# Expert blocks of 448 rows for 512, with half-array matmuls for the leftovers, in a fused recurrent and mixture-of-experts kernel

## The chip, the cores and the metric

The kernel runs on one core of a Trainium2 chip. The metric is the device time of one execution in microseconds. Three runs of the kernel before gave 911.64, 923.08 and 937.19 us, median 923.08 us.

## The reference

A recurrent attention block (RWKV-7) runs over 768 steps for 4 batches of 8 heads of 40 dimensions, and its output is taken as 3072 rows of 320. A mixture of 8 experts follows, in which each row goes to one expert.

```python
def _attn_ref(r, k, v, w, a, b):
    ...
    for t in range(S):
        ...
        y[:, :, t] = np.einsum('bhd,bhde->bhe', rt, state)
        Sa = np.einsum('bhde,bhe->bhd', state, at)
        state_decay = state * wt[:, :, None, :] - np.einsum('bhd,bhe->bhde', Sa, bt)
        state = state_decay + np.einsum('bhd,bhe->bhde', vt, kt)
    ...
def _moe_ref(x, w_gate, w1, w2):          # x (3072, 320), w1 (8, 320, 1024), w2 (8, 1024, 320)
    ...
    expert_idx = np.argmax(logits, axis=1)
    ...
        h = np.maximum(x_sorted[lo:hi] @ w1[e], 0.0)
        y_sorted[lo:hi] = h @ w2[e]
    ...
    return (gate_w[:, None] * y)
```

## The kernel before

All data are fp32. The program has three stages.

*Recurrent stage.* The 768 steps are cut into 12 chunks of 64. Each chunk is a chain of small matmuls that use the TensorE array as quarter tiles of 64 x 64 (helper `mm`, L222). The orders of TensorE, VectorE and ScalarE are written out by hand (`weave`); GpSimd and the DMA queues are ordered by the scheduler. At the end of a chunk `emit` multiplies the chunk's outputs by an identity and the gate weights (`ps_x`); ScalarE copies the result to `xr` in two halves (L552), and the sync queue writes 64-row pieces of `xr` to a scratch tensor `x_rows` in memory, 320 columns and one more for the gate weight (L562).

*Routing stage.* VectorE turns the logits into an expert for each row and a slot within the expert. Each expert owns `NJ` = 4 blocks of 128 rows, so its capacity is 512; rows past that go to overflow blocks. A one-hot matmul (`tok_ps`) inverts the slots to lists of row numbers (`g_idx`, `s_idx`), which indirect DMAs on GpSimd use.

*Expert stage.* For each expert: `gather` fetches four blocks of 128 rows from `x_rows` (`xg`, L822); `turn` transposes them on TensorE, three column blocks of 128, 128 and 64 columns (`tp`, L832), with a VectorE copy after each (L833); `layer1` computes eight feature blocks of 128 features, each as three accumulating matmuls over 128, 128 and 64 contraction rows with 512 columns (`hp`, L841), and VectorE and ScalarE take turns at the ReLU (L846, L848); `layer2` makes four output blocks of eight accumulating matmuls of 320 columns (`zp`, L854), ScalarE scales each by the gate weight (`zo`, L859), and GpSimd scatters it to the output (L860). Two experts' weights are in SBUF at a time; `fetch` reads expert e + 2 after expert e is done (L687 w1's first 256 rows, L689 its last 64, L690 w2). The scheduler sets the order of this stage. A last loop handles overflow blocks, as many as the routing has counted.

Of the kernel before, what the change touches and what calls it, by code (L numbers as in the profile page):

```python
# [8 lines left out]
F32 = mybir.dt.float32  # L9
# [12 lines left out]
def kernel(  # L22
# [29 lines left out]
    dch = [(d0, min(128, Dm - d0)) for d0 in range(0, Dm, 128)]  # L52
    DB = len(dch)


    NJ = 4
    CAP = NJ * 128
    NX = -(-(N - CAP) // 128)
    NC = E * NJ + NX
    assert NC <= 128  # L60

# [24 lines left out]
    b1off = counted("b1off", [128, E], [[CAP, E]], -1, 0)  # L86
    b2off = counted("b2off", [128, E], [[-CAP, E]], E * CAP - CAP, 0)
# [28 lines left out]
    x_d = nc.dram_tensor("x_rows", (N, Dm + 1), F32, kind="Internal").ap()  # L116


    with tc.tile_pool(name="ring", bufs=1) as ring, \
# [421 lines left out]
        def emit(us):  # L541
# [3 lines left out]
            xr = sb.tile([128, NB2, NP, 2, D], F32, name="xr", bufs=2)  # L545
            lg = sb.tile([128, 2, NB2, E], F32, name="lg", bufs=2)
            for par, ps in enumerate(pss):
                def end():
# [3 lines left out]
                    nc.scalar.copy(xr[:, :, :, par].rearrange("t s p e -> t (s p) e"), ps[:, :, :, :D].rearrange("t s p e -> t (s p) e"))  # L552
# [143 lines left out]
    with tc.tile_pool(name="rps", bufs=1, space=PSUM) as rps_pool:  # L696
# [9 lines left out]
        xw = x_d[:, Dm : Dm + 1].rearrange("(s b c t) o -> b s t (c o)", b=2, t=64, s=B // 2)  # L706
# [39 lines left out]
        nc.vector.scalar_tensor_tensor(b2[:], in0=b2[:], scalar=128.0, in1=b2off[:], op0=ALU.mult, op1=ALU.add)  # L746
# [16 lines left out]
        nc.vector.tensor_scalar(gx[:], slot[:], scalar1=CAP + 0.5, scalar2=None, op0=ALU.is_ge)  # L763
        nc.vector.tensor_tensor(gx[:], gx[:], b2[:].unsqueeze(2).to_broadcast([128, E, NT]), op=ALU.mult)
# [52 lines left out]
    mps_pool = ctx.enter_context(tc.tile_pool(name="moe_ps", bufs=3, space=PSUM))  # L817

    def gather(g):
        g["xg"] = xg_pool.tile([128, NJ, Dm + 1], F32, name="xg")  # L820
        for j in range(g["n"]):
            nc.gpsimd.indirect_dma_start(  # L822
                out=g["xg"][:, j, :], out_offset=None,
                in_=x_d[:, :], in_offset=bass.IndirectOffsetOnAxis(ap=g["gi"](j), axis=0),
            )

    def turn(g):
        g["xT"] = wk_pool.tile([128, DB, CAP], F32, name="xgT")
        for j in range(g["n"]):
            tp = mps_pool.tile([128, DB, 128], F32, name="tp", bufs=2)  # L830
            for db, (d0, dsz) in enumerate(dch):
                nc.tensor.transpose(tp[:dsz, db, :], g["xg"][:, j, d0 : d0 + dsz], ident[:])  # L832
                nc.vector.tensor_copy(g["xT"][:dsz, db, j * 128 : (j + 1) * 128], tp[:dsz, db, :])  # L833

    def layer1(g):
        cols = g["n"] * 128
        g["h"] = wk_pool.tile([128, FB, CAP], F32, name="h_sb")
        for fb in range(FB):
            hp = mps_pool.tile([128, CAP], F32, name="hp")
# [97 lines left out]
```

## Time and profile before

| | before |
|---|---|
| time, median of three runs | 923.08 us |
| the profiled execution's own time | 923.31 us |
| its span, first to last instruction | 921.6 us |
| TensorE matmuls busy | 793.9 us (86%) |
| TensorE weight loads busy | 599.7 us (65%) |
| VectorE, ScalarE, GpSimd busy | 343.7, 286.2, 368.0 us |
| mean granted TensorE clock | 0.953 of 2.4 GHz |
| mean DMA traffic | 65 GB/s |

The span is one execution seen by the profiler; the time adds what lies before and after it. A matmul's record has a modelled end, so the distance between the starts of two records says more than their durations. One fp32 matmul of the program makes two records, each with its weight load.

### The profile page before, as it was taken

How to read it: one execution, taken by the hardware profiler on the slowest of the kernel's cores; microseconds unless marked ns; L12 is line 12 of the kernel's file. 1: busy time of each engine (PE TensorE's matmuls, PEld its weight loads, DVE VectorE, ACT ScalarE, POOL GpSimd, SP SyncE). 2: the span in 40 equal slices, each digit the busy share in tenths (PEclk: the TensorE clock that was granted, in tenths of full speed). 3: DMA queues.
4: the chain of work that ended last, by engine and by line, in shares of the span. 5: the costliest groups of instructions: out<-in, count | busy, mean ns of one | idle time of the engine just before them, and what ended most of it. 6: DMA issues, size and time to landing. Idle time of an engine off the chain costs nothing.

```text
span 921.6 us, 37467 instructions
## 1 busy us (share of the span) xinstructions
PE 793.9 (86%) x16828; PEld 599.7 (65%) x16828; DVE 343.7 (37%) x645; ACT 286.2 (31%) x756; POOL 368.0 (40%) x436
## 2 busy tenths in 40 slices
PE   0678989898889888888889854999999999999995
PEld 0577988798888788887879852364544545363633
DVE  2467273817374555738363235112010101011100
ACT  0245355435546354554646420101111001111010
POOL 9566355634565555556573326020302021210101
PEclk9999699959999999999999985999999999999998
DMA  4213322312223222322110038032313132221000
GB/s 96 63 40 68 71 45 67 72 45 51 63 62 74 47 62 58 68 61 58 35 33 19 11 74 244 22 142 81 104 65 101 65 100 72 91 80 59 21 0 22
DMA packets 119605, 60.16 MB, mean 65 GB/s; under 512 B 103825, under 2 KB 115091, under 8 KB 119444
## 3 DMA queue, kind: packets, MB, share of 16 engines
q1 hardware_dynamic: 109156, 47.55, 19.9%
q0 software_dynamic: 3072, 9.20, 3.2%
q8 instruction: 133, 2.18, 1.0%
q10 hardware_dynamic: 7216, 1.00, 0.7%
q14 instruction: 28, 0.23, 0.1%
HBM read 49.83 MB, written 9.19 MB: 64 GB/s over the span
## 4 chain that ended last, share of the span: by engine, by line
PE 43%; issue 38%; POOL 9%; DVE 4%; DMA 3%; ACT 1%; SPq 0%; POOLq 0%; DVEq 0%; ACTq 0%
PE ps_lv L222 9%; PE ps_y L222 5%; PE ps_ntb L222 4%; PE ps_q L222 4%; POOL out_dram L860 3%; PE ps_atv L222 3%; PE ps_gtk L222 3%; PE ps_f L222 3%; PE ps_z L222 3%; PE ps_x L222 3%; POOL xg L822 2%; PE ps_S L222 2%; PE ps_uT L222 2%; PE ps_s L222 2%; POOL kb L284 1%
## 5 line engine op out<-in xcount | busy, mean ns | idle before, releaser
L222 PE MATMUL ps_lv<-pair,N 64*64 64x96 f32 (+2 forms) x3840 | 200.3, 243 | 27.4 <-issue 17.9
L222 PEld LDWEIGHTS ps_lv<-pair,N 64*64 64x64 f32 x3840 | 170.3, 137 | 32.9 <-issue 23.1
L841 PE MATMUL hp<-xgT,w 128*128 128x512 f32 (+1 forms) x384 | 191.3, 628 | 0.0
L854 PE MATMUL zp<-w,h_sb 128*128 128x320 f32 x512 | 145.0, 433 | 0.0
L841 PEld LDWEIGHTS hp<-xgT,w 128*128 128x128 f32 (+1 forms) x384 | 63.1, 189 | 122.9 <-issue 120.6
L860 POOL DMA_INDIRECT out_dram<-zo,s_idx x32 | 31.8, 993 | 278.3 <-ACT zo L859 251.2
L854 PEld LDWEIGHTS zp<-w,h_sb 128*128 128x128 f32 x512 | 94.6, 191 | 34.5 <-issue 0.8
L846 DVE TENSOR_SCALAR h_sb<-hp 128x512 f32<-128x512 f32 x32 | 22.1, 692 | 246.5 <-PE hp L841 246.5
L335 DVE STREAM_TRANSPOSE N<-pair 128x512 f32<-128x512 f32 x120 | 84.0, 700 | 64.2 <-ACT pair L385 63.0
L284 POOL TENSOR_TENSOR kb<-kb,wi 128x256 f32<-128x256 f32 x96 | 68.8, 737 | 55.2 <-DVE wi L281 47.7
L222 PE MATMUL ps_ntb<-ai,kb 40*64 40x104 f32 x768 | 64.0, 292 | 28.7 <-POOL ai L275 26.6
L281 DVE RECIPROCAL wi<-PT 128x128 f32<-128x128 f32 x96 | 88.0, 921 | 0.1
L848 ACT ACTIVATE h_sb<-hp 128x512 f32<-128x512 f32 x32 | 19.1, 597 | 198.7 <-PE hp L841 198.7
L385 ACT COPY pair<-ps_lv 128x512 f32<-128x512 f32 x96 | 56.7, 590 | 73.9 <-PE ps_lv L222 58.6
L222 PEld LDWEIGHTS ps_ntb<-ai,kb 40*64 40x64 f32 x768 | 47.3, 157 | 29.2 <-POOL ai L275 26.6
L859 ACT ACTIVATE zo<-zp,xg 128x320 f32<-128x320 f32 x32 | 16.9, 528 | 131.9 <-PE zp L854 128.2
L361 POOL TENSOR_TENSOR pair<-pair 128x256 f32<-128x256 f32 x24 | 17.5, 727 | 89.9 <-DVE pair L355 89.9
L222 PE MATMUL ps_f<-TT,xt 64*64 64x64 f32 x768 | 50.0, 249 | 1.4 <-POOL TT L393 0.9
L549 DVE TENSOR_REDUCE lg<-ps_x 128x16 f32<-128x64 f32 x24 | 5.4, 225 | 118.4 <-PE ps_x L222 115.8
L275 POOL TENSOR_TENSOR ai<-a,PT 128x512 f32<-128x512 f32 x24 | 28.4, 1182 | 51.0 <-DVE PT L271 41.3
L222 PE MATMUL ps_gtk<-ai,kb 40*64 40x104 f32 x768 | 45.4, 262 | 2.4 <-issue 2.4
L222 PE MATMUL ps_atv<-ri,v 40*64 40x104 f32 x768 | 42.2, 255 | 4.9 <-issue 3.9
(170 smaller groups left out, 1548.8 us busy)
## 6 DMA issues: line engine op xcount, KB each, us to landing
w<-in_moe_w_dram SPq DMA_DIRECT2D x8, 1280.0 KB
w<-in_moe_w_dram SPq DMA_DIRECT2D x8, 1024.0 KB
kb<-in_packed_dram SPq DMA_DIRECT2D x176, 40.0 KB
v<-in_packed_dram SPq DMA_DIRECT2D x96, 40.0 KB
wp<-in_packed_dram SPq DMA_DIRECT2D x96, 40.0 KB
ri<-in_packed_dram SPq DMA_DIRECT2D x96, 40.0 KB
x_rows<-xr SPq DMA_DIRECT2D x48, 80.0 KB
a<-in_packed_dram SPq DMA_DIRECT2D x88, 40.0 KB
```

What stands on the lines that cost most here:

```text
L222: nc.tensor.matmul(out_, lhsT=lhs, rhs=rhs, start=start, stop=stop, skip_group_check=free)
L275: nc.gpsimd.tensor_tensor(by_batch(d["ai"][:, :, :T2]), d["a"][:], by_batch(PT[:, :, :T2]), op=ALU.mult,)
L281: nc.vector.reciprocal(wi[:, h, p : p + 2], by_batch(d["PT"][:, :, 1:])[:, h, p : p + 2])
L284: nc.gpsimd.tensor_tensor(d["kb"][:, h, i], d["kb"][:, h, i], wi[:, h], op=ALU.mult)
L335: nc.vector.transpose(N[:].rearrange("q g a t -> q a g t"), nt)
L385: nc.scalar.copy(parts(new[:, :2]), ps[:, :, :T2].rearrange("q g (a t) -> q g a t", a=2))
L822: nc.gpsimd.indirect_dma_start(out=g["xg"][:, j, :], out_offset=None, in_=x_d[:, :], in_offset=bass.IndirectOffsetOnAxis(ap=g["gi"](j), ax ...
L841: nc.tensor.matmul(hp[:, :cols], lhsT=g["w"][0][:dsz, db, fb * 128 : (fb + 1) * 128], rhs=g["xT"][:dsz, db, :cols], start=(db == 0), stop= ...
L846: nc.vector.tensor_relu(g["h"][:, fb, :cols], hp[:, :cols])
L848: nc.scalar.activation(g["h"][:, fb, :cols], hp[:, :cols], AF.Relu)
L854: nc.tensor.matmul(zp[:], lhsT=g["h"][:, fb, j * 128 : (j + 1) * 128], rhs=g["w"][1][:, fb, :], start=(fb == 0), stop=(fb == FB - 1),)
L860: ins_ = nc.gpsimd.indirect_dma_start(out=out[:, :], out_offset=bass.IndirectOffsetOnAxis(ap=g["si"](j), axis=0), in_=zo[:], in_offset=Non ...
```

## The change

An expert now owns three blocks of 128 rows and half a block of 64, so its capacity is 448. The half blocks of two neighbouring experts share one gathered block (`xs`, 128 rows: 64 of each), and the routing has one more step for the slots from 385 to 448. Four things follow.

- `x_rows` is 384 columns wide: its last 64 features stand twice, so that a transposed block has them on partitions 0 to 63 and again on 64 to 127. GpSimd makes the second copy in `xr` before it is written.
- `turn` makes three transposes of 128 columns into one PSUM tile and one VectorE copy of all 384 columns; a shared block is copied in two parts, 64 rows to each expert's `xgT`.
- `layer1` handles feature blocks in pairs with 448 columns. The last 64 contraction rows run as two matmuls, one block on row half 0 to 63 and the other on 64 to 127, into two PSUM banks (`rest`). They come first in pairs 0 and 2 and last in pairs 1 and 3. The weights for them are a tile of their own (`w1r`), with the two blocks' weights on the two halves.
- `layer2` runs for three own blocks, and after every second expert once for the shared block: two matmuls per feature block, one for each expert's 64 rows, with outputs on partitions 0 to 63 and 64 to 127. For this h and w2 have three buffers instead of two.

```diff
-    NJ = 4
-    CAP = NJ * 128
+    NJ = 3
+    OWN = NJ * 128
+    CAP = OWN + 64
+    NO = E * NJ + E // 2
...
+                    nc.gpsimd.tensor_copy(xr[:, :, Dm:], xr[:, :, Dm - 64 : Dm])
                     for s in range(NB2):
                         for b2 in range(2):
...
-                                x_d[r0 : r0 + T2, :Dm], xr[b2 * 64 : b2 * 64 + 64, s].rearrange("t p a e -> t (p a e)"),
+                                x_d[r0 : r0 + T2, :DX], xr[b2 * 64 : b2 * 64 + 64, s],
...
+        t1 = w_pool.tile([128, DF, F], F32, name="w1")
+        tr = w_pool.tile([128, FB // 2, 128], F32, name="w1r")
+        t2 = w_pool.tile([128, FB, Dm], F32, name="w2", bufs=3)
+        for half in range(2):
+            nc.sync.dma_start(
+                tr[half * 64 : half * 64 + 64], w1[DF * 128 :].rearrange("r (q a x) -> a r q x", a=2, x=128)[half],
+            )
...
-        nc.vector.tensor_scalar(gx[:], slot[:], scalar1=CAP + 0.5, scalar2=None, op0=ALU.is_ge)
-        nc.vector.tensor_tensor(gx[:], gx[:], b2[:].unsqueeze(2).to_broadcast([128, E, NT]), op=ALU.mult)
+        gy = sm_pool.tile([128, E, NT], F32)
+        for t, cap, to in ((gx, OWN, b2off), (gy, CAP, b2)):
+            nc.vector.scalar_tensor_tensor(
+                t[:], in0=slot[:], scalar=cap + 0.5, in1=to[:].unsqueeze(2).to_broadcast([128, E, NT]), op0=ALU.is_ge, op1=ALU.mult,
+            )
+        nc.vector.tensor_add(gx[:], gx[:], gy[:])
...
+    def turn(xg, j, *to):
+
+        tp = mps_pool.tile([128, DB, 128], F32, name="tp")
+        for db in range(DB):
+            nc.tensor.transpose(tp[:, db, :], xg[:, j, db * 128 : db * 128 + 128], ident[:])
+        n = 128 // len(to)
+        for i, (xT, c0) in enumerate(to):
+            nc.vector.tensor_copy(xT[:, :, c0 : c0 + n], tp[:, :, i * n : i * n + n])
+
+    def layer1(xT, w, cols):
+        h = wk_pool.tile([128, FB, CAP], F32, name="h_sb", bufs=3)
+        for q in range(FB // 2):
+            hps = [mps_pool.tile([128, CAP], F32, name="hp", bufs=4) for _ in range(2)]
+
+            def rest():
+                for a in range(2):
+                    rows = slice(a * 64, a * 64 + 64)
+                    nc.tensor.matmul(
+                        hps[a][:, :cols], lhsT=w[1][rows, q, :], rhs=xT[rows, DF, :cols], start=(q % 2 == 0), stop=(q % 2 == 1),
+                    )
+
+            if q % 2 == 0:
+                rest()
+            for a in range(2):
+                f0 = (2 * q + a) * 128
+                for db in range(DF):
+                    nc.tensor.matmul(
+                        hps[a][:, :cols], lhsT=w[0][:, db, f0 : f0 + 128], rhs=xT[:, db, :cols],
+                        start=(q % 2 == 1 and db == 0), stop=(q % 2 == 0 and db == DF - 1),
+                    )
+            if q % 2 == 1:
+                rest()
+            nc.vector.tensor_relu(h[:, 2 * q, :cols], hps[0][:, :cols])
+            nc.scalar.activation(h[:, 2 * q + 1, :cols], hps[1][:, :cols], AF.Relu)
+        return h
+
+    def layer2(parts, weight, idx, apart):
+
+        zp = mps_pool.tile([128, Dm], F32, name="zp")
+        n = 128 // len(parts)
         for fb in range(FB):
...
+            for i, (h, w, c0) in enumerate(parts):
                 nc.tensor.matmul(
...
+                    zp[i * n : i * n + n], lhsT=h[:, fb, c0 : c0 + n], rhs=w[2][:, fb, :], start=(fb == 0), stop=(fb == FB - 1),
                 )
...
+    for e in range(E):
+        p = e // 2
         if e + 2 < E:
...
+            if e % 2 == 0:
+                gather_shared(p + 1)
+            gather_own(e + 2)
+        hs[e] = layer1(xTs[e], weights[e], CAP)
         if e + 1 < E:
...
+            if e % 2 == 1:
+                turn_shared(p + 1)
+            turn_own(e + 1)
+        for j in range(NJ):
+            layer2([(hs[e], weights[e], j * 128)], own[e][:, j, DX:], s_idx[:, e * NJ + j : e * NJ + j + 1], True)
+        if e % 2 == 1:
+            layer2(
+                [(hs[i], weights[i], OWN) for i in (e - 1, e)], shared[p][:, 0, DX:],
+                s_idx[:, E * NJ + p : E * NJ + p + 1], True,
+            )
         if e + 2 < E:
             weights[e + 2] = fetch(moe_w1[e + 2], moe_w2[e + 2])
```

How the instructions stand on an engine is the scheduler's work, so three places are shown. A row names the line, the operation, output and inputs, the shape and a repeat count.

TensorE, from the transposes within expert 2's layer two to expert 3's layer one, before (`xg` into `tp` are transposes, `h_sb` into `zp` layer two, `xgT` into `hp` layer one):

```order
L832 MATMUL tp<-ident,xg 128x128 x2
L854 MATMUL zp<-w_11625,h_sb 128x320
L832 MATMUL tp<-ident,xg 128x128 x2
L854 MATMUL zp<-w_11625,h_sb 128x320
L832 MATMUL tp<-ident,xg 64x128 x2
L854 MATMUL zp<-w_11625,h_sb 128x320 x27
L841 MATMUL hp<-xgT,w_11760 128x512 x24
```

And with the change, expert 3's layer one, the transposes for expert 4 (a shared block `xs` and three own blocks) and its own layer two:

```order
L859 MATMUL hp<-xgT,w1r 128x448 x2
L868 MATMUL hp<-xgT,w_11752 128x448 x8
L859 MATMUL hp<-xgT,w1r 128x448 x4
L868 MATMUL hp<-xgT,w_11752 128x448 x8
L859 MATMUL hp<-xgT,w1r 128x448 x2
L846 MATMUL tp<-ident,xs 128x128 x3
L846 MATMUL tp<-ident,xg 128x128 x3
L884 MATMUL zp<-w_11754,h_sb 128x320
L846 MATMUL tp<-ident,xg 128x128 x3
L884 MATMUL zp<-w_11754,h_sb 128x320
L846 MATMUL tp<-ident,xg 128x128 x3
L884 MATMUL zp<-w_11754,h_sb 128x320 x22
```

The 64-row matmuls (L859) now stand as 2, 4 and 2 instead of one in each feature block, the transposes in threes with fewer layer-two matmuls between them, and behind these rows come 16 of the shared block's layer two (`zp`, 64x320), which alternate between expert 2's and expert 3's half.

The sync queue, from the last chunks' writes of `x_rows` to the end of the first weight fetches, before:

```order
L562 DMA x_rows<-xr_10054 64x320 x4
L562 DMA x_rows<-xr_10937 64x320 x4
L687 DMA w1_11315<-in_moe_w1_dram 128x2x1024
L562 DMA x_rows<-xr_11265 64x320 x4
L689 DMA w1_11315<-in_moe_w1_dram 64x1024
L690 DMA w2_11316<-in_moe_w2_dram 128x8x320
L687 DMA w1_11320<-in_moe_w1_dram 128x2x1024
L689 DMA w1_11320<-in_moe_w1_dram 64x1024
L690 DMA w2_11321<-in_moe_w2_dram 128x8x320
```

And with the change (`w1r` is the tile for the last 64 rows):

```order
L570 DMA x_rows<-xr_10951 64x384 x4
L696 DMA w1r_11332<-in_moe_w1_dram 64x4x128 x2
L570 DMA x_rows<-xr_11280 64x384 x4
L699 DMA w1_11331<-in_moe_w1_dram 128x2x1024
L700 DMA w2_11333<-in_moe_w2_dram 128x8x320
L696 DMA w1r_11339<-in_moe_w1_dram 64x4x128 x2
L699 DMA w1_11338<-in_moe_w1_dram 128x2x1024
L700 DMA w2_11340<-in_moe_w2_dram 128x8x320
L700 DMA w2_11615<-in_moe_w2_dram 128x8x320
```

The large w1 piece of expert 0 moved behind the last writes, the small piece ahead of them, and a third w2 joined the first two experts' weights.

GpSimd, at the end of one chunk and the beginning of the next, with the change (`AT` belongs to the chunk's masks, `pair` to the next chunk's first system); before, the same rows stand there without the copy:

```order
L542 TENSOR_TENSOR y<-y,PT_3115 128x512
L330 TENSOR_TENSOR AT_5260<-AT_5260,up_161 128x512
L330 TENSOR_TENSOR AT_5300<-AT_5300,up_161 128x512
L566 COPY xr<-xr 128x2x64
L367 TENSOR_TENSOR pair_5520<-pair_5516 128x256
L368 TENSOR_TENSOR pair_5520<-pair_5520,i_150 128x256
L367 TENSOR_TENSOR pair_5575<-pair_5571 128x256
```

The copy of `xr` came in between the masks and the pair additions.

## Rows read from the trace of the kernel before

**Rows 1.** Table of stretches: busy us per engine (instructions), PEclk, DMA share, GB/s.

```profile
552.00:578.00 26.00, 11.35 (x45) 5.52 (x46) 13.87 (x36) 0.00 (x0) 16.90 (x16) 0.55 0.80 230
704.00:746.00 42.00, 42.00 (x124) 20.55 (x124) 5.69 (x16) 4.51 (x8) 7.50 (x9) 1.00 0.27 86
872.00:921.60 49.60, 39.50 (x109) 19.17 (x108) 2.77 (x4) 4.50 (x8) 4.35 (x5) 0.95 0.03 10
```

**Rows 2.** Page, section 5: the two matmul lines of the expert stage.

```profile
L841 PE MATMUL hp<-xgT,w 128*128 128x512 f32 (+1 forms) x384 | 191.3, 628 | 0.0
L854 PE MATMUL zp<-w,h_sb 128*128 128x320 f32 x512 | 145.0, 433 | 0.0
```

**Rows 3.** Timeline of the sync queue: start, us, then two of the six fetches.

```profile
682.46 0.37 SPq L687 DMA_DIRECT2D w<-in_moe_w_dram  x1
724.78 0.37 SPq L687 DMA_DIRECT2D w<-in_moe_w_dram  x1
```

**Rows 4.** Timeline of PEld: one feature block of layer one, the next's start.

```profile
712.81 0.30 PEld L841 LDWEIGHTS hp<-xgT,w 128*128 128x128 f32 x2 [0.76 <-issue]
713.35 0.19 PEld L841 LDWEIGHTS hp<-xgT,w 128*128 128x128 f32 x1 [0.24 <-issue]
713.78 0.19 PEld L841 LDWEIGHTS hp<-xgT,w 128*128 128x128 f32 x1 [0.24 <-issue]
714.73 0.29 PEld L841 LDWEIGHTS hp<-xgT,w 64*128 64x128 f32 x2 [0.76 <-issue]
715.78 0.30 PEld L841 LDWEIGHTS hp<-xgT,w 128*128 128x128 f32 x2 [0.76 <-issue]
```

**Rows 5.** Timeline of PE, layer two of one expert and what follows it.

```profile
728.85 14.70 PE L854 MATMUL zp<-w,h_sb 128*128 128x320 f32 x54
743.39 6.95 PE L841 MATMUL hp<-xgT,w 128*128 128x512 f32 x14
```

**Rows 6.** Groups of PE by line and shape in the microsecond from 460 us.

```profile
L222 PE MATMUL ps_lv<-pair,N 64*64 64x96 f32 x28 | 1.5, 252 | 0.0
L222 PE MATMUL ps_z<-ri,uT 40*64 40x104 f32 x27 | 1.4, 249 | 0.0
```

**Rows 7.** Timeline of PE, the last chunk's ps_x, first half.

```profile
540.38 0.67 PE L222 MATMUL ps_x<-iw,y 40*64 40x48 f32 x16 [0.17 <-POOL y L536]
```

**Rows 8.** Timeline of VectorE: one routing step, one ReLU, two copies after transposes.

```profile
551.01 0.36 DVE L765 TENSOR_TENSOR slot<-slot,gx 128x192 f32<-128x192 f32 x1
...
721.82 0.69 DVE L846 TENSOR_SCALAR h_sb<-hp 128x512 f32<-128x512 f32 x1 [5.24 <-PE hp L841]
725.05 0.49 DVE L833 COPY xgT<-tp 128x128 f32<-128x128 f32 x2 [2.54 <-PE tp L832]
```

**Rows 9.** DMA view, 563 to 566 us: packets, MB, share; issues, us to landing.

```profile
q1 hardware_dynamic: 776, 0.99, 105.4%
...
xg<-x_rows,g_idx POOLq DMA_INDIRECT x3, 3.8
```

**Rows 10.** DMA view, 566 to 569 us, the same columns.

```profile
q0 software_dynamic: 157, 0.56, 57.4%
q1 hardware_dynamic: 212, 0.25, 22.8%
```

**Rows 11.** Timeline of PE at the start of the expert stage.

```profile
567.99 4.18 PE L832 MATMUL tp<-ident,xg 128*128 128x128 f32 x10 [6.70 <-DMA xg<-x_rows,g_idx]
...
574.38 6.22 PE L841 MATMUL hp<-xgT,w 128*128 128x512 f32 x11
```

**Rows 12.** Timelines of ScalarE and GpSimd after one chunk's last output copy.

```profile
364.71 0.43 ACT L552 COPY xr<-ps_x 128x320 f32<-128x320 f32 x1 [0.18 <-DVE lg L549]
...
367.40 0.73 POOL L361 TENSOR_TENSOR pair<-pair 128x256 f32<-128x256 f32 x1 [4.95 <-DVE pair L355]
```

**Rows 13.** Table of stretches, two in the recurrent stage.

```profile
100.00:104.00 4.00, 4.00 (x78) 4.00 (x78) 0.40 (x2) 1.49 (x4) 0.42 (x1) 0.50 0.02 4
188.00:192.00 4.00, 4.00 (x81) 4.00 (x80) 0.00 (x0) 1.72 (x5) 1.74 (x2) 0.50 0.38 86
```

More of the change, by code (lines that the diff above doesn't have):

```diff
@@ L113 @@
     lmin = rte.tile([128, NT], F32)
-    x_d = nc.dram_tensor("x_rows", (N, Dm + 1), F32, kind="Internal").ap()
+    x_d = nc.dram_tensor("x_rows", (N, DX + 1), F32, kind="Internal").ap()
     with tc.tile_pool(name="ring", bufs=1) as ring, \
@@ L816, with gather @@
     wk_pool = ctx.enter_context(tc.tile_pool(name="moe_wk", bufs=2))
[L817 to L821, printed above, removed]
+    mps_pool = ctx.enter_context(tc.tile_pool(name="moe_ps", bufs=2, space=PSUM))
+    def gather(idx, n, name):
+        xg = xg_pool.tile([128, n, DX + 1], F32, name=name)
+        for j in range(n):
             nc.gpsimd.indirect_dma_start(
-                out=g["xg"][:, j, :], out_offset=None,
-                in_=x_d[:, :], in_offset=bass.IndirectOffsetOnAxis(ap=g["gi"](j), axis=0),
-            )
@@ L827, in turn @@
[L827 to L837, printed above, removed]
+                out=xg[:, j, :], out_offset=None,
@@ new lines, in layer2 @@
+        zo = wk_pool.tile([128, Dm], F32, name="zo", bufs=3)
+        nc.scalar.activation(zo[:], zp[:], AF.Copy, scale=weight)
+        ins_ = nc.gpsimd.indirect_dma_start(
+            out=out[:, :], out_offset=bass.IndirectOffsetOnAxis(ap=idx, axis=0),
+            in_=zo[:], in_offset=None, bounds_check=N - 1, oob_is_err=False,
+        )
+        ins_ = getattr(ins_, "ins", ins_)
+        if apart:
+            tc.declare_no_dep(ins_, group="rows_out", reason="disjoint rows")
+            tc.add_to_no_dep_group("rows_out", ins_)
@@ L869, in cols_of, with gather_own, gather_shared @@
     def cols_of(t, c0):
         return lambda j: t[:, c0 + j : c0 + j + 1]
-    groups = [dict(n=NJ, gi=cols_of(g_idx, e * NJ), si=cols_of(s_idx, e * NJ), apart=True) for e in range(E)]
-    gather(groups[0])
-    gather(groups[1])
-    turn(groups[0])
-    for e, g in enumerate(groups):
+    own, shared, xTs, hs = {}, {}, {}, {}
+    def gather_own(e):
+        own[e] = gather(cols_of(g_idx, e * NJ), NJ, "xg")
+    def gather_shared(p):
+        shared[p] = gather(cols_of(g_idx, E * NJ + p), 1, "xs")
@@ L877, with turn_own, turn_shared @@
+    def turn_own(e):
+        for j in range(NJ):
+            turn(own[e], j, (xTs[e], j * 128))
+    def turn_shared(p):
+        for e in (2 * p, 2 * p + 1):
+            xTs[e] = wk_pool.tile([128, DB, CAP], F32, name="xgT", bufs=3)
+        turn(shared[p], 0, (xTs[2 * p], OWN), (xTs[2 * p + 1], OWN))
+    gather_shared(0)
+    gather_own(0)
+    gather_own(1)
+    turn_shared(0)
+    turn_own(0)
+    for e in range(E):
+        p = e // 2
         if e + 2 < E:
-            gather(groups[e + 2])
@@ L879 @@
-        g["w"] = weights.pop(e)
-        layer1(g)
+            if e % 2 == 0:
+                gather_shared(p + 1)
+            gather_own(e + 2)
+        hs[e] = layer1(xTs[e], weights[e], CAP)
         if e + 1 < E:
-            turn(groups[e + 1])
-        layer2(g)
+            if e % 2 == 1:
+                turn_shared(p + 1)
+            turn_own(e + 1)
+        for j in range(NJ):
+            layer2([(hs[e], weights[e], j * 128)], own[e][:, j, DX:], s_idx[:, e * NJ + j : e * NJ + j + 1], True)
@@ L897 @@
             )
-            g = dict(n=1, w=w, gi=lambda j: gi[:, 0:1], si=lambda j: gi[:, 1:2], apart=False)
-            gather(g)
-            turn(g)
-            layer1(g)
-            layer2(g)
+            xg = gather(lambda j: gi[:, 0:1], 1, "xs")
+            xT = wk_pool.tile([128, DB, CAP], F32, name="xgT", bufs=3)
+            turn(xg, 0, (xT, 0))
+            h = layer1(xT, w, 128)
+            layer2([(h, w, 0)], xg[:, 0, DX:], gi[:, 1:2], False)
 _OUTS = [((3072, 320), 'float32')]
```

67 lines of the change are left out of this document (21 added, 46 removed).

## The prediction

> **What bounds the kernel now.** I read the table by stage first. From 578 to 912 us, the expert stage, TensorE is busy in every microsecond at a granted clock of 1.00, while VectorE, ScalarE and GpSimd are busy for 5.7, 4.5 and 7.5 of 42 us and the DMA engines for 0.27 of it [rows 1]. Six starts of a weight fetch stand 42.3 us apart, one expert each [rows 3]: eight experts fill 339 of the 921.6 us, and each is a chain of TensorE work with nobody else late. So here columns streamed are time, and the page's two costly groups say which ones: 384 records of layer one and 512 of layer two [rows 2], two records for each fp32 matmul (8 x 24 and 8 x 32 matmuls). The recurrent stage before it is not touched but for one copy.
>
> Next, the price of one record. In layer one the weight loads of a feature block start at 712.81, 713.35, 713.78, 714.73 and the next block at 715.78 [rows 4]: 0.43 us from one 512-column record to the next, 2.97 us a block. Six records are 6 x 0.43 = 2.57 us, so 0.39 us of each block is lost at the two places where the loads change between 128 and 64 rows: 0.2 us a change. In layer two 54 records of 320 columns lie between 728.85 and 743.39: 0.269 us each [rows 5]. Both are 0.84 ns a column. One expert is then 8 x 2.97 = 23.7 (layer one) + 64 x 0.269 = 17.2 (layer two) + 1.4 us of transposes, the rest of 42.3.
>
> **The change, part by part.** (a) *Layer one, 448 columns for 512.* A record becomes 448/512 x 0.43 = 0.376 us. The 32 records that contract all 128 rows cost 12.0 us. (b) *The last 64 rows.* Sixteen records on 64 rows now come as pairs, one on each row half. If a pair takes the time of one: 8 x 0.376 = 3.0 us; if the halves run one after the other, 6.0. The expert stage of before has no such pair, but the recurrent stage has a stricter case: in the microsecond from 460 us, 55 records of 96 and 104 columns overlap [rows 6]. Taking off the 10 or so that began before it, 45 x some 84 ns = 3.8 us of streaming was done in 1.0 us, so four quarter tiles ran at once, among them tiles that share their columns and differ in rows. I take 3.0. (c) *Fewer changes of shape.* The order gathers the 64-row records of the second and third pair of blocks, so an expert has 6 changes for 16: 1.2 us. Layer one: 12.0 + 3.0 + 1.2 = 16.2 for 23.7.
>
> (d) *Layer two.* Three own blocks are 48 x 0.269 = 12.9 us. The shared block is 32 records for two experts, in two column halves. As pairs they are 16 x 0.269 = 4.3 us, one after the other 8.6; a change of shape adds 0.2. The row for column halves of the same rows is ps_x: 16 records of 48 columns in 0.67 us [rows 7], of which some 0.22 is the tail of the last. That is 7 steps of 0.06 us for pairs, where two records alone would need 0.08 and a perfect pair 0.04. With such short records I put the missing 0.02 down to the weight loads, which a 0.269 us record covers, and take 4.3; half of 4.5 is 2.25 us an expert. Layer two: 15.2 for 17.2.
>
> (e) *Transposes.* 10.5 for 12 an expert, no longer cut to 64 columns, and one copy for three. A copy of 384 columns lies between those of 128 (0.245 us) and 512 (0.69) [rows 8], about 0.57; with two buffers the third turn may wait 0.2 us for the first copy behind the last ReLU. I leave the 1.4 us as they are (1.0 to 2.2).
>
> One expert: 16.2 + 15.2 + 1.4 = 32.8 us, a gain of 9.6, eight times 76.6. What might be late next is not: weights are 2.6 MB an expert, at the 0.33 MB/us seen in [rows 9] 8 us out of 32.8; VectorE and ScalarE keep about 5 us each, and GpSimd issues 7 transfers for 8.
>
> (f) *Start of the expert stage.* The third w2 buffer lets the sync queue issue expert 2's w2 (1.31 MB) with the first weights, and the big part of expert 0's w1 (1.05 MB) now stands behind the last x_rows writes, where a 0.26 MB part stood. So 2.1 MB more lie in the hardware queue when the first gather is issued at 563. In the trace that queue (q1) moved 0.99 MB in the 3 us after 563 and the gathers' queue (q0) has no line there [rows 9]; their packets appear only in the next 3 us, when the weights end with 0.25 MB [rows 10], and the first transpose waits for them until 567.99 [rows 11]. If gathers stand behind weights, they come 2.1/0.33 = 6.4 us later. Against that, the turns that took from 567.99 to 574.38, before layer one streams [rows 11], have six copies instead of twelve, about 4 us instead of 6.4. The sum lies between -2.4 (gathers not held) and +6 (held, and the turns no faster); I take +4, as [rows 9] and [rows 10] say that they are held. The Trainium skill (DMA: Bandwidth & Descriptors, Queues, rings and completion order) says that each DMA engine goes round between the queues that have work, packet by packet; by that the gathers would not be held, and the total would be some 6 us lower; [rows 9] does not agree.
>
> (g) *Recurrent stage.* Twelve GpSimd copies of 128 columns, each behind ScalarE's xr copy, with the pair add queued behind it. After one xr copy ends at 365.14, GpSimd idles until 367.40 [rows 12], and the gap is 2.1 us or more in all twelve chunks, against some 0.4 us for a copy (half of a 256-column operation of 0.73 there). The writes of x_rows wait for it, but nobody waits for those until the gathers. Zero; uncovered it would be 12 x 0.4 = 5 us. (h) *Routing.* Three VectorE operations on 192 columns for two, 0.36 us each [rows 8]: +0.4. The overflow loop stays empty: the reference's own inputs give each expert 323 to 423 rows, and the new capacity is 448.
>
> **Sum.** The profiled execution took 923.31 us (span 921.6 and 1.7 around it), 0.2 above the median of the three runs, so I sum against it: 923.3 - 76.6 + 4 + 0.4 = **851 us**.
>
> **Rivals.** *Row halves do not overlap.* The 64-row pairs would cost 3.0 us more an expert: 851 + 24 = 875. For it: no 64 x 128 pair stands in the trace, and both halves feed all 128 columns. Against it: [rows 6]. *Column halves do not overlap:* 4.3 us more for each of four shared blocks, 868; for it, that both halves read the same rows; against it, [rows 7]. *Halves overlap in part.* If the 1.5 of [rows 7] (0.06 for 0.04) holds for long records too, the shared blocks cost 2.15 x 4 = 8.6 and the row pairs 1.5 x 8 = 12 us more: 872. For it: it is the only row of this very form. Against it: [rows 6], and the weight loads explain it. Of this rival the Trainium skill has a measured case (TensorE: Matmul & The Clock Gate, Measured speedup vs the span model): four row tiles gave 3.07 instead of 4. An estimate by that ratio, a pair at 1.3 of one record, is 863; no run here shows it for long records.
>
> *Slower: the clock.* The recurrent stage, which runs on half and quarter tiles, has stretches at a granted clock of 0.50 (1.2 GHz) with TensorE busy in all of it [rows 13]; the expert stage held 1.00 on full tiles. If its half-tile parts made the clock fall, each microsecond of full-speed work at half clock costs one more. Of the stage's 260 us, 72 at half clock eat the gain and some 90 make the kernel over 2% slower (941 or more); all of it would give over 1100. Against it: only 5.3 of 32.8 us an expert are half tiles, in pairs that fill the array.
>
> **How the numbers follow.** The forecast as worked out has 0.79, the row rival 0.05, the column rival 0.05, partial overlap 0.07, the slow clock 0.02, and 0.02 something that leaves the time within 2%. Around 851 the forecast's own spread is the start term (-6 to +2), the turns (-3 to +6), and above all the recurrent stage: the profiled run has two stretches of 20 us or more at half clock, of which [rows 13] shows 4 us each, and one more or fewer moves a run by some 10 us, as the three runs from 912 to 937 show. That makes 836 to 866 for it. Held to 8 in 10, with most of the column case: **836 to 869**. A measurement of this kernel can tell about 2% from no change; faster by more than that (below 905): 0.96, within 2%: 0.02, slower: 0.02.
>
> **What the profile after would show.** Weight fetches of experts about 32.8 us apart, on the mean of an odd and an even one (30.5 and 35). In layer one 448-column records 0.376 us apart, and in the 64-row parts two starts within some 10 ns and then 0.376 us. If those starts stand alone at 0.376, the row rival is right. In the shared block, two 320-column starts every 0.269 us; 0.4 speaks for partial overlap. Between the blocks, no TensorE wait over 0.3 us except at the third turn. At the start, the first transpose near 574 and layer one streaming from about 578; if it comes at 568, (f) was wrong. GpSimd's xr copy must end before the pair add would have started. The forecast fails if the stage is still 40 us an expert, if TensorE waits for the gather or the weights in each expert, or if PEclk in the expert stage is below 1.00.

## The result and the profile after

The changed kernel took 846.87 us in the median of four runs (836.65 to 850.72), the kernel before 927.85 us in the four beside them (911.64 to 937.19). The ratio is 0.919 with a 95% interval of 0.898 to 0.941: faster. In two further sets of runs it was 0.910 (0.901 to 0.920; medians 831.01 and 909.39 us) and 0.912 (0.907 to 0.918; 828.54 and 911.01 us). The forecast was 851 us, in a range of 836 to 869.

The profiled execution after took 844.75 us (span 843.0), against 923.31 before: 78.6 us less. The first view is the page's list of groups: line, operation, busy us and mean ns of one record, idle time before.

```profile
L884 PE MATMUL zp<-w,h_sb 128*128 128x320 f32 (+1 forms) x512 | 124.1, 433 | 0.0
...
L868 PE MATMUL hp<-xgT,w 128*128 128x448 f32 x256 | 101.4, 549 | 0.0
```

Layer two has the 512 records that it had before [rows 2], and yet 21 us less busy time at the same 433 ns of one: 128 of them, those of the four shared blocks, now run in pairs. Layer one's full-row records are 256, of 448 columns for 512. To see where an expert's time goes, I read the timeline of TensorE over two experts in the steady stage; columns are start, us, line, operation, count.

```profile
639.83 1.02 PE L859 MATMUL hp<-xgT,w1r 64*128 64x448 f32 x4
640.78 6.28 PE L868 MATMUL hp<-xgT,w 128*128 128x448 f32 x16
646.99 1.77 PE L859 MATMUL hp<-xgT,w1r 64*128 64x448 f32 x8
648.69 6.28 PE L868 MATMUL hp<-xgT,w 128*128 128x448 f32 x16
654.90 1.02 PE L859 MATMUL hp<-xgT,w1r 64*128 64x448 f32 x4
655.86 0.87 PE L846 MATMUL tp<-ident,xg 128*128 128x128 f32 x6
656.57 0.70 PE L884 MATMUL zp<-w,h_sb 128*128 128x320 f32 x2
657.11 0.54 PE L846 MATMUL tp<-ident,xg 128*128 128x128 f32 x3
657.49 12.55 PE L884 MATMUL zp<-w,h_sb 128*128 128x320 f32 x46
669.96 1.02 PE L859 MATMUL hp<-xgT,w1r 64*128 64x448 f32 x4
...
685.04 1.02 PE L859 MATMUL hp<-xgT,w1r 64*128 64x448 f32 x4
...
688.57 16.47 PE L884 MATMUL zp<-w,h_sb 128*128 128x320 f32 x76
704.97 1.02 PE L859 MATMUL hp<-xgT,w1r 64*128 64x448 f32 x4
```

No row carries an idle time, and no record starts more than 0.48 us behind the one before it: TensorE waits for nobody. Layer one lasts from 639.83 to 655.86, 16.0 us (forecast 16.2). Eight 64-row records take 1.77 us and four 1.02, so the four between them cost 0.75: two steps of 0.376 us for two pairs (the two starts of a pair lie 7 ns apart, as the trace has them). In layer two 46 own records last 12.55 us; at the end of the odd expert 76 records, 44 own and 32 of the shared block, last 16.47. The 44 are 44 x 0.269 = 11.8 us, and the shared block has 4.6 left (forecast 4.5 with its change of shape). The sync queue's fetches show the same in whole experts; before, they stood 42.3 us apart [rows 3].

```profile
655.00 0.37 SPq L699 DMA_DIRECT2D w<-in_moe_w_dram  x1
...
685.14 0.37 SPq L699 DMA_DIRECT2D w<-in_moe_w_dram  x1
...
720.15 0.37 SPq L699 DMA_DIRECT2D w<-in_moe_w_dram  x1
...
750.29 0.37 SPq L699 DMA_DIRECT2D w<-in_moe_w_dram  x1
```

They are 30.14, 35.01 and 30.14 us apart: 32.6 an expert in the mean (forecast 30.5 and 35.0, mean 32.8). The table of stretches gives the clock and the other engines over these two experts, in the columns of [rows 1].

```profile
639.83:704.97 65.14, 65.14 (x247) 36.60 (x246) 8.60 (x16) 8.05 (x15) 13.81 (x15) 1.00 0.38 118
```

TensorE is busy in all of it at 1.00 (2.4 GHz), and nobody else is near: in these two experts the slow clock of the prediction did not come, and no wait took the place of the streamed columns.

The start of the expert stage is where forecast and trace part. Below are TensorE's timeline there, the table of stretches from layer one's first record to 577 us, the gathers' rows of GpSimd, then the DMA view of 561 to 564 us and that of 564 to 567 us (packets, MB, share; issues, us to landing).

```profile
568.65 0.88 PE L846 MATMUL tp<-ident,xs 128*128 128x128 f32 x3 [8.70 <-DMA w<-in_moe_w_dram]
...
573.31 1.87 PE L859 MATMUL hp<-xgT,w1r 64*128 64x448 f32 x4
```

```profile
573.31:577.00 3.69, 3.69 (x8) 1.58 (x8) 0.56 (x1) 0.00 (x0) 2.78 (x4) 0.50 0.63 164
```

```profile
562.28 1.19 POOL L836 DMA_INDIRECT xs<-x_rows,g_idx  x1 [2.79 <-DMA w<-in_moe_w_dram]
563.77 0.95 POOL L836 DMA_INDIRECT xg<-x_rows,g_idx  x1 [0.30 <-issue]
```

```profile
q1 hardware_dynamic: 848, 1.09, 106.3%
...
xs<-x_rows,g_idx POOLq DMA_INDIRECT x1, 6.3
```

```profile
q1 hardware_dynamic: 862, 1.09, 107.3%
```

The gathers are held behind weights, as forecast: q0 has no line in either view, and the first gather lands 6.3 us after its issue. But the first transpose comes at 568.65, where I had put 574, and layer one streams from 573.31, where I had put 578; before, these were 567.99 and 574.38 [rows 11]. That row leaves out what ran between the two:

```profile
572.11 2.05 PE L841 MATMUL hp<-xgT,w 128*128 128x512 f32 x2
```

Two records of layer one stood before the last two transposes (at 573.95), so before, 1.84 us of layer one's work lay ahead of 574.38. Both kernels begin layer one at a granted clock of 0.50: after until 577.0, before from 572.11 to 575.5. The weights named behind "<-" can't be what was waited for: this transpose reads gathered rows alone, and a gather reads none of the weights.

Last, the recurrent stage: GpSimd's new copy behind one chunk's xr copy.

```profile
360.52 0.29 POOL L566 COPY xr<-xr 128x128 f32<-128x128 f32 x1 [2.12 <-ACT xr L559]
362.72 0.73 POOL L367 TENSOR_TENSOR pair<-pair 128x256 f32<-128x256 f32 x1 [1.91 <-DVE pair L361]
```

The copy takes 0.29 us, and after it GpSimd still waits 1.91 us for VectorE. It lies in the gap of [rows 12] and costs nothing.

The 78.6 us split at two marks, the last normalized logits on VectorE and the start of layer one's streaming. The recurrent stage up to the first mark ends 1.65 us earlier (542.27 for 543.92), the start takes 31.04 us for 30.46, and the expert stage to the end of the span 269.7 for 347.2: -1.65 + 0.58 - 77.53 = -78.6. With the 1.84 us of layer one counted in both kernels to the expert stage, the start is 2.4 us longer and the expert stage 79.4 us shorter.

### The profile page after: what moved, and what is told of

The parts are those of the page before. It is cut to its first block, busy times and chain, and to the rows that moved or that the text cites. A ratio compares the mean times of both kernels' runs of the same rounds, so it can differ in the third digit from the quotient of the medians.

```text
span 843.0 us, 37380 instructions
## 1 busy us (share of the span) xinstructions
PE 709.9 (84%) x16816; PEld 576.3 (68%) x16816; DVE 332.9 (39%) x582; ACT 282.6 (34%) x752; POOL 364.4 (43%) x442
## 3 DMA queue, kind: packets, MB, share of 16 engines
q8 instruction: 133, 2.18, 1.1%
## 4 chain that ended last, share of the span: by engine, by line
PE 48%; issue 35%; POOL 7%; DVE 4%; DMA 4%; ACT 1%; SPq 1%; POOLq 0%; ACTq 0%; DVEq 0%
PE ps_lv L228 11%; PE ps_y L228 6%; PE ps_ntb L228 5%; PE ps_q L228 4%; PE ps_atv L228 4%; PE ps_gtk L228 3%; POOL out_dram L889 3%; PE ps_f L228 3%; PE ps_z L228 3%; PE ps_x L228 3%; PE ps_S L228 2%; PE ps_uT L228 2%; PE ps_s L228 2%; POOL xg L836 1%; DMA w<-in_moe_w_dram 1%
## 5 line engine op out<-in xcount | busy, mean ns | idle before, releaser
L884 PE MATMUL zp<-w,h_sb 128*128 128x320 f32 (+1 forms) x512 | 124.1, 433 | 0.0
L889 POOL DMA_INDIRECT out_dram<-zo,s_idx x28 | 27.9, 998 | 210.3 <-ACT zo L888 209.7
L884 PEld LDWEIGHTS zp<-w,h_sb 128*128 128x128 f32 (+1 forms) x512 | 80.5, 177 | 37.1 <-issue 2.4
L874 DVE TENSOR_SCALAR h_sb<-hp 128x448 f32<-128x448 f32 x32 | 20.0, 625 | 209.3 <-PE hp L868 132.3
L868 PE MATMUL hp<-xgT,w 128*128 128x448 f32 x256 | 101.4, 549 | 0.0
L228 PE MATMUL ps_ntb<-ai,kb 40*64 40x104 f32 x768 | 62.4, 288 | 28.9 <-POOL ai L281 26.9
L868 PEld LDWEIGHTS hp<-xgT,w 128*128 128x128 f32 x256 | 47.8, 192 | 53.1 <-issue 53.1
L875 ACT ACTIVATE h_sb<-hp 128x448 f32<-128x448 f32 x32 | 17.4, 544 | 142.8 <-PE hp L868 87.6
L888 ACT ACTIVATE zo<-zp,xg 128x320 f32<-128x320 f32 x24 | 12.7, 528 | 100.0 <-PE zp L884 100.0
L228 PEld LDWEIGHTS ps_f<-TT,xt 64*64 64x64 f32 x768 | 42.0, 144 | 2.8 <-issue 1.1
```

The costliest lines, as they stand in the source:

```text
L228: nc.tensor.matmul(out_, lhsT=lhs, rhs=rhs, start=start, stop=stop, skip_group_check=free)
L868: nc.tensor.matmul(hps[a][:, :cols], lhsT=w[0][:, db, f0 : f0 + 128], rhs=xT[:, db, :cols], start=(q % 2 == 1 and db == 0), stop=(q % 2 == ...
L874: nc.vector.tensor_relu(h[:, 2 * q, :cols], hps[0][:, :cols])
L875: nc.scalar.activation(h[:, 2 * q + 1, :cols], hps[1][:, :cols], AF.Relu)
L884: nc.tensor.matmul(zp[i * n : i * n + n], lhsT=h[:, fb, c0 : c0 + n], rhs=w[2][:, fb, :], start=(fb == 0), stop=(fb == FB - 1),)
L888: nc.scalar.activation(zo[:], zp[:], AF.Copy, scale=weight)
```

## The experiments

Totals of this kernel move by 10 us and more between executions. The reading that does not is the expert stage: from layer one's first record to the end of the span it took 269.7, 269.9 and 269.7 us in the three traces of the changed kernel, while their spans were 843.0, 830.8 and 830.3. So each experiment is read by that length and by the spacing of its fetches, and totals stand beside.

**Row halves.** Both matmuls of a 64-row pair run on row half 0 to 63:

```diff
-        tr = w_pool.tile([128, FB // 2, 128], F32, name="w1r")
+        tr = w_pool.tile([64, 2, FB // 2, 128], F32, name="w1r")
...
-                tr[half * 64 : half * 64 + 64], w1[DF * 128 :]...
+                tr[:, half], w1[DF * 128 :]...
...
-                    rows = slice(a * 64, a * 64 + 64)
+                    rows = slice(0, 64)
...
-                        hps[a][:, :cols], lhsT=w[1][rows, q, :], ...
+                        hps[a][:, :cols], lhsT=w[1][rows, a, q, :], ...
```

> Both 64-row matmuls of each pair on row half 0 to 63 (the second half's weights and columns are read from there too); the output is then another one. Theory (row halves run at the same time, a pair for 0.376 us): the pair parts now need 16 records in turn for 8, +3.0 us an expert; fetch starts 33 and 38 us apart for 30.1 and 35.0, total +24, about 869. In the records, the two starts of a pair 0.376 us apart for 0.007. Rival (the gain of layer one comes from the columns and the order alone, the halves run in turn anyway): spacing unchanged, about 845.

The computation is the whole one, other than this says: xgT holds the last 64 columns in both row halves. The timeline of TensorE over one layer one:

```profile
664.51 1.77 PE L859 MATMUL hp<-xgT,w1r 64*128 64x448 f32 x4
666.21 6.28 PE L868 MATMUL hp<-xgT,w 128*128 128x448 f32 x16
672.42 3.27 PE L859 MATMUL hp<-xgT,w1r 64*128 64x448 f32 x8
675.62 6.28 PE L868 MATMUL hp<-xgT,w 128*128 128x448 f32 x16
681.83 1.77 PE L859 MATMUL hp<-xgT,w1r 64*128 64x448 f32 x4
```

The pair parts, 1.02, 1.77 and 1.02 us in the changed kernel, are 1.77, 3.27 and 1.77: 3.0 us more, and nothing else moved. The spacing is 33.1 and 37.95, and the stage 294.3 us, 24.6 longer, for 24 expected (the single total is 854.07 us, beside 904.41 of the kernel before). The theory holds to the 0.376 us step; the rival falls.

**Column halves.** In the shared block one expert's 8 matmuls come before the other's:

```diff
-        for fb in range(FB):
-            for i, (h, w, c0) in enumerate(parts):
+        for i, (h, w, c0) in enumerate(parts):
+            for fb in range(FB):
```

> In the shared block the 8 matmuls of one expert's column half come before the other's 8, no longer by turns; the output is the same. Theory (column halves overlap only because the two records stand next to each other): +4.3 us for each of four shared blocks, odd spacing 39 for 35.0, even 30.1, total +17, about 862. Rival (the halves do not overlap in the changed kernel, or overlap whatever the order): spacing unchanged, about 845.

This run took 985.09 us, and its table of stretches says why it can't be used: the first stretch lies in the recurrent stage, which the edit doesn't touch, the second in the expert stage.

```profile
100.00:400.00 300.00, 299.97 (x8776) 297.21 (x8772) 151.68 (x251) 140.96 (x382) 151.18 (x163) 0.65 0.26 58
...
640.00:940.00 300.00, 300.00 (x832) 142.22 (x831) 28.60 (x53) 27.36 (x51) 39.47 (x40) 0.75 0.22 71
```

So the kernel was run again, in four executions:

> The kernel with the column halves of the shared block in turn, once more, as its first run had a granted clock of about 0.7 from the recurrent stage on (985 us). Theory (the low clock belonged to that run, since it began 500 us before the changed block): granted clock about 0.96, odd spacing 39.3 for 35.0, even 30.1, total +17 on the changed kernel of the same chip. Rival (the order in turn brings the low clock with it): again 0.7 and 950 or more, in most of the executions. Rival on the halves: odd spacing unchanged at 35.0.

The granted clock was 1.00 this time (575 to 743 us of the profiled execution), and no execution came near the 985 us: that rival falls. From the timeline of TensorE, then of the table of stretches for zp alone (us, TensorE busy and records, weight loads busy and records; then ScalarE, clock, DMA):

```profile
677.13 19.75 PE L884 MATMUL zp<-w,h_sb 128*128 128x320 f32 x76
```

```profile
691.00:692.00 1.00, 1.00 (x5) 0.55 (x4) 0.00 (x0) 1.00 0.44 164
692.30:693.30 1.00, 1.00 (x9) 0.67 (x8) 0.00 (x0) 1.00 0.29 60
694.00:695.00 1.00, 1.00 (x5) 0.55 (x4) 0.00 (x0) 1.00 0.66 148
```

The 76 records take 19.75 us for 16.47. Odd spacing is 38.28, even 30.14, the stage 283.0 us, 13.3 longer: the column halves overlap in the changed kernel, and to alternate them saves 3.28 us a block. That is 1.0 less than the 4.3 expected, and the table shows where it is: about four weight loads begin in a microsecond in the middle of either half, but eight at the seam. There the second expert's first four records run beside the first's last four, 4 x 0.269 = 1.08 us, though the kernel's text has them behind (the order in which the scheduler put them on the engine is not on record for this run). The total was 853.87 us in the median beside 828.54 of the changed kernel on that chip, more than 13.3 explains; its executions had a mean granted clock of 0.946 to 0.970 against 0.963 to 0.976. What made up the rest, and what set the low clock of the first run, stays open.

**Changes of shape.** The 64-row pair always stands first in its pair of feature blocks:

```diff
-                        ..., start=(q % 2 == 0), stop=(q % 2 == 1),
+                        ..., start=True, stop=False,
...
-            if q % 2 == 0:
-                rest()
+            rest()
...
-            if q % 2 == 1:
-                rest()
```

> The pair of 64-row matmuls stands first in each of the four pairs of feature blocks: 8 changes between 128 and 64 rows an expert for 6 within layer one. Theory (0.2 us a change): +0.4 us an expert, fetch starts about 30.5 and 35.4 apart, total +3. Rival (the 0.2 us belongs to 64-row records that stand alone and not to the change): nothing, 30.1 and 35.0.

The fetches of two experts, big part of w1 again:

```profile
655.34 0.37 SPq L699 DMA_DIRECT2D w<-in_moe_w_dram  x1
...
685.88 0.37 SPq L699 DMA_DIRECT2D w<-in_moe_w_dram  x1
...
721.28 0.37 SPq L699 DMA_DIRECT2D w<-in_moe_w_dram  x1
```

30.54 and 35.40 us: +0.40 and +0.39, two changes of 0.2 us each. The stage is 273.0, 3.3 longer for 3.2 expected; the rival falls (the single total is 845.95 us).

**The two parts alone.** One kernel has the row-half pairs with four own blocks of 128 rows, the other the 448 columns and the shared block with layer one's order as it was. The first also has the old routing and two buffers of w2 and h, which go with four blocks:

```diff
-    NJ = 3
+    NJ = 4
     OWN = NJ * 128
-    CAP = OWN + 64
-    NO = E * NJ + E // 2
+    CAP = OWN
+    NO = E * NJ
...
```

```diff
...
+        for fb in range(FB):
+            hp = mps_pool.tile([128, CAP], F32, name="hp", bufs=4)
+            for db in range(DB):
+                r = 128 if db < DF else 64
+                nc.tensor.matmul(
+                    hp[:, :cols], lhsT=w[0][:r, db, fb * 128 : (fb + 1) * 128], rhs=xT[:r, db, :cols],
+                    start=(db == 0), stop=(db == DB - 1),
+                )
...
```

> Only the layer-one part of the change: row-half pairs and their grouping, with four own blocks of 128 rows an expert (512 columns), no shared block. Theory by the terms of the sum at 512 columns: 32 records x 0.43 = 13.7, 8 pairs x 0.43 = 3.4, 6 changes 1.2, layer two 17.2, turns 1.4: 36.9 us an expert for 42.3, total 923 - 8 x 5.4 = 880. Rival (pairs run in turn): 40.3 us an expert, about 907.

> Only the other part: three and a half blocks (448 columns) with the shared block in column halves; layer one's last 64 rows as before, one 64-row matmul within each feature block. Theory by the terms: 48 records x 0.376 = 18.0, 16 changes 3.2, layer two 15.2, turns 1.4: 37.8 us an expert for 42.3, total 923 - 8 x 4.5 = 887. Rival (column halves run in turn): 40.0 us, about 905.

> The changed kernel once more on this chip, for the comparison with its two parts: 845 +- 10 us, spacing 30.1 and 35.0. The two parts' gains should add up to the whole's, but for what they share: 43 (pairs) + 36 (blocks) against 77, as 448 columns also shorten the pairs and the pairs shorten the 448 columns.

Fetch starts of the pairs alone, then of the blocks alone:

```profile
706.96 0.37 SPq L698 DMA_DIRECT2D w<-in_moe_w_dram  x1
...
744.07 0.37 SPq L698 DMA_DIRECT2D w<-in_moe_w_dram  x1
```

```profile
659.11 0.47 SPq L694 DMA_DIRECT2D w<-in_moe_w_dram  x1
...
694.15 0.47 SPq L694 DMA_DIRECT2D w<-in_moe_w_dram  x1
...
734.25 0.47 SPq L694 DMA_DIRECT2D w<-in_moe_w_dram  x1
```

Pairs alone: 37.11 us an expert (36.9 expected). Blocks alone: 35.04 and 40.10, 37.6 in the mean (37.8). Both rivals, 40.3 and 40.0, fall. Totals are 866.69 and 875.68 us in the median beside 909.39 before and 831.01 after (the 845 +- 10 expected for the last was too high, as the kernel before took 14 us less here than in the runs that the forecast was made from), ratios to before 0.953 (0.944 to 0.961) and 0.961 (0.949 to 0.974). The pairs save 5.2 us an expert and the blocks 4.7, together 9.9, and the whole 9.7. What they share is then 0.2 us; by the terms it should be 0.43, 8 x (0.43 - 0.376), as the pairs stream 448 columns only in the whole. I did not follow the difference.

**The start.** Expert 2's w2 is taken out of the first weights, with two buffers for three; in a second kernel expert 1's weights also go out on GpSimd's queue behind the first gathers:

```diff
-        t2 = w_pool.tile([128, FB, Dm], F32, name="w2", bufs=3)
+        t2 = w_pool.tile([128, FB, Dm], F32, name="w2")
```

```diff
...
-    weights = {e: fetch(moe_w1[e], moe_w2[e]) for e in range(2)}
+    weights = {0: fetch(moe_w1[0], moe_w2[0])}
...
     gather_own(1)
+    weights[1] = fetch(moe_w1[1], moe_w2[1], nc.gpsimd)
     turn_shared(0)
```

> w2 has two buffers for three, so expert 2's w2 is not among the first weights but is fetched when expert 0 is done. Theory for the start of the expert stage (gathers are held behind what is left on the hardware queue): 1.3 MB less is in front of them, about 4 us at 0.33 MB an us; the first transpose comes near 565 for 568.65, if the x_rows writes end at the same time. Rival (only some 5 us of holding whatever is queued): first transpose within 1 us of 568.65. In the steady stage both expect the even and odd spacing unchanged at 30.1 and 35.0 while the fetch of w2 (4 us) has 30 us to land; if spacing grows, the third buffer hides a wait.

> Expert 1's weights go out on GpSimd's queue behind the first three gathers, and w2 has two buffers; only expert 0's weights are on the hardware queue when the gathers are issued. Theory (gathers wait for the queued weights): first transpose 3 to 4 us earlier than 568.65, total about -3. Rival (holding does not depend on what is queued): no change at the start. Price to watch in both: expert 1's weights must land by about 603, some 40 us after their issue.

With two w2 buffers, the first gather on GpSimd, then on TensorE the first transposes and those of the fifth block:

```profile
545.42 1.19 POOL L836 DMA_INDIRECT xs<-x_rows,g_idx  x1 [2.43 <-DVE s_idx L826]
```

```profile
549.23 0.87 PE L846 MATMUL tp<-ident,xs 128*128 128x128 f32 x3 [5.78 <-DMA xs<-x_rows,g_idx]
...
553.91 0.87 PE L846 MATMUL tp<-ident,xg 128*128 128x128 f32 x3 [0.39 <-DMA xg<-x_rows,g_idx]
```

And the DMA view of 547 to 550 us there:

```profile
q0 software_dynamic: 139, 0.45, 58.2%
q1 hardware_dynamic: 35, 0.04, 3.6%
```

The first transpose begins 3.8 us after the gather's issue, against 6.4, 5.9 and 5.2 in the three traces of the changed kernel: 1.31 MB less is worth 1.4 to 2.6 us of holding, not the 4 expected. The second kernel shows why no more was to be had. There the hardware queue is empty when the first gather is issued, and the transpose still comes 3.7 us behind it: that is what a gather takes here with nothing in front.

From the last normalized logits to layer one it is 28.9 us against 31.0, 30.0 and 31.7; the single total is 826.01 us. Of what the first transpose gained, part is lost again: the gathers are issued 1.25 us apart, and once they are not held, each block's transposes wait for its own gather, down to the fifth block's in the row above (the turns take 5.5 us for 4.7). Spacing is 30.14 and 35.01 as expected, the stage 269.5, so the third buffer hides nothing here. In the second kernel the gathers were issued 21.3 us after the logits (20.0, 22.4 and 20.0 in the three traces of the changed kernel, 19.6 with two buffers), and layer one begins after 30.5. Nothing is won: 829.91 us in the median beside 831.01.

**A version meant to beat both.** Two w2 buffers, and layer one over 424 columns:

```diff
-    CAP = OWN + 64
+    CAP = OWN + 40
...
-    b3off = counted("b3off", [128, E], [[-64, E]], E * 64 - 64, 0)
+    b3off = counted("b3off", [128, E], [[-64, E]], E * 64 - 40, 0)
...
-        h = wk_pool.tile([128, FB, CAP], F32, name="h_sb", bufs=3)
+        h = wk_pool.tile([128, FB, OWN + 64], F32, name="h_sb", bufs=3)
+        if cols == CAP:
+            nc.gpsimd.memset(h[:, :, CAP:], 0.0)
```

> A version meant to beat both: layer one over 424 columns for 448 (the fullest expert of these inputs has 423 rows; beyond 424 the overflow loop takes them), the 24 unused columns of h set to zero by GpSimd, and two w2 buffers for three. Theory (column streaming sets the expert): 24 x 0.84 ns x 40 record times = 0.8 us an expert, spacing 29.3 and 34.2, 6.4 us in all; with the start some 2 us earlier as with two w2 buffers alone, 8 us or 1.0% below the changed kernel. Rival (a part of each record does not go by its columns, or the ReLUs and buffers end last): spacing gain under 0.4 us.

> The changed kernel on the same chip and in the same rounds, to stand beside the two others: spacing 30.1 and 35.0, ratio to before about 0.91 to 0.92.

```profile
664.78 0.37 SPq L699 DMA_DIRECT2D w<-in_moe_w_dram  x1
...
698.96 0.37 SPq L699 DMA_DIRECT2D w<-in_moe_w_dram  x1
...
728.27 0.37 SPq L699 DMA_DIRECT2D w<-in_moe_w_dram  x1
```

These fetch starts are 34.18 and 29.31 us apart, 0.83 less each, as 24 columns at 0.84 ns ask. The stage is 263.9 us, 5.8 shorter for 6.4 expected (layer one's first 5.2 us ran at a granted clock of 0.50, its first 3.7 in the run beside), and it starts 28.6 us after the logits for 30.0. The totals say less: 824.87 us in the median (ratio to before 0.909, 0.904 to 0.914) beside 828.54 (0.912, 0.907 to 0.918). The traces say 7 us of gain, the medians 3.7, and the intervals overlap. It is faster than the kernel before; that it beats the changed kernel is shown in the stage that it changes and not in the totals.

## Why the prediction was right, and where it was off

- **(a) and (b), layer one's columns and pairs.** The 448-column records stream in 0.376 us, and a pair of row halves takes the time of one record. Shown by the timeline after, and by the run on one row half, which cost the 3.0 us an expert that the row rival was priced at.
- **(c) Changes of shape.** 0.2 us each, shown by two more of them costing 0.40. Layer one came to 16.0 for 16.2.
- **(d) Layer two.** The shared block takes 4.6 us for 4.5. The column rival falls with the run in turn; its price, 4.3 us, was too high by the 1.0 that the halves still overlap at the seam. The partial overlap is out too: [rows 7] gave 1.5 for short records, and the stage lost nothing of it with records of 0.269 us. The Trainium skill (TensorE: Matmul & The Clock Gate, Measured speedup vs the span model) has four row tiles at 3.07 instead of 4; here two row tiles of 448 columns give 2.
- **(e) Transposes.** The expert's remainder is 32.6 less layer one's 16.0 and layer two's 15.2 (12.9 and half of 4.6): 1.4 us, as taken. No turn waited in the two experts shown.
- **(f) The start: the term that was mis-sized.** "I take +4" came to +2.1 for the same work (the 2.4 above less the routing), and by the prediction's own sign, a first transpose at 568, (f) was wrong. The mechanism was there: the gathers stand behind the hardware queue. The step that failed is that "2.1 MB more lie in the hardware queue when the first gather is issued". The DMA view from that issue on, 563 to 575 us before and 562.28 to 574 us after, has what was left in the queue (packets, MB, share):

```profile
q1 hardware_dynamic: 988, 1.24, 32.0%
```

```profile
q1 hardware_dynamic: 1640, 2.06, 52.0%
```

It is 0.8 MB more. Of the 2.1, 0.8 was expert 0's w1 piece, which only changed places: before, it was issued at 543.77 us, 0.15 ahead of the last logits, and went out ahead of the gathers too. Of the 1.4 MB that were really added (w2 and the wider rows), 0.6 had already been moved (4.89 MB between the logits and the first gather for 4.33). So the first transpose came 6.4 us after the gather's issue for 5.0, +1.4 and not +6.4.

The turns were to save 2.4 us by six copies for twelve. The 6.4 us that the prediction read from [rows 11] hold the two records of layer one, so twelve transposes took 4.55; after, they took 3.83 (568.65 to 572.48), 0.7 less, and then the scheduler had put three transposes of expert 1's first block ahead of layer one, 0.8 us. The first gather left 0.6 us later behind its row numbers. Together 1.4 - 0.7 + 0.8 + 0.6 = 2.1.

How long a gather is held follows from what is left at its issue. In the thirteen traces kept, its first packet (q0) came 1.76 us after the issue with an empty hardware queue, 1.89 with 0.52 MB left, 2.50 with 1.14, 3.27 with 1.24 (before), 3.81 with 1.55 and 4.79 with 2.06, and always when q1 had at most 0.32 MB to go. The Trainium skill (DMA: Bandwidth & Descriptors, Queues, rings and completion order) has each DMA engine go round packet by packet between the queues that have work; in the six microseconds from 561 there are 2.18 MB of q1 and no packet of q0, though a gather was issued at 562.28. That does not agree, unless the gather's packets were not yet in their queue, which no trace here shows.

- **(g) and (h).** The GpSimd copy is hidden: behind it GpSimd waits 1.8 us or more in each of the ten chunks whose pair additions come next. The routing's +0.4 measured +0.3: the row numbers (`g_idx`) are ready 19.1 us after the logits for 18.8 before, and for 18.8 in the run of the pairs alone, which has the old routing.
- **Clock.** 1.00 in the two experts shown, 0.50 in layer one's first 3.7 us (3.4 before). Until the last matmul the other low stretches lay in the recurrent and the routing stage, where they moved totals by 10 us and more, as forecast: the last logits came at 542.3 us in the profiled run after, with 0.50 from 181 to 205 us among others, and at 529.2 and 530.6 in the two other traces of the changed kernel, which have no low stretch from 110 to 530 us.

The profiled run came 6.4 us under the sum: 2.8 in the expert stage (79.4 for 76.6: 1.4 by the spacing, 1.0 behind the last matmul, which the sum did not have, 0.4 by the block turned ahead, as the first fetch spacing is 29.76 us for 30.14), 2.0 at the start with the routing (+2.4 for +4.4), 1.6 in the recurrent stage. All three lie on one side. That the total fell within the range owes something to luck all the same, since the recurrent stage moves it by more than that: in the two other sets of runs both kernels were faster, the changed one with 831.01 and 828.54 us under the range's lower end, while the gain was 78.4 and 82.5 us (78.6 in the profiled runs) for the 72 forecast.

## What to carry to other kernels

Where one engine is busy in every microsecond of a stage, price the change in records by the step from one start to the next: forecast and trace then agree to 0.2 us an expert. A matmul that contracts 64 rows, or writes 64 columns, left half of the array free here, and a second one of 448 or 320 columns on the other half, next to it, took no time of its own (16 of 48 columns overlapped only in part [rows 7]); each switch between tile shapes cost 0.2 us, so such matmuls belong together. Before pricing a queue by the bytes that a change adds, count what is left in it when the transfer in question is issued: 0.8 MB here, not 2.1. Where totals scatter by more than the effect, compare the length of the one stage and its spacing in the traces.

## What was not expected of the hardware

- Matmuls on different column halves overlapped though they were not next to each other in the kernel's text: at the seam of the run in turn the second expert's first four records ran beside the first's last four (eight weight loads begun in one microsecond for four, 1.0 us won).
- A whole execution had a granted clock at neither of the two levels, 1.2 and 2.4 GHz: 0.65 in the recurrent stage and 0.75 in the expert stage, with 76 layer-two records of the run in turn in 25.76 us for 19.75. A second profiled run of the same kernel had 0.970 in the mean. What set it is not known.
